# Both pieces of the products of rows 9 to 12 side by side in the fixed opening list of a retention and feed-forward kernel

## The chip, the cores and the metric

The kernel runs on one core of a Trainium2 chip. A core has five engines, each with an instruction stream of its own that it works through in order: PE (TensorE, the matrix products), DVE (VectorE), ACT (ScalarE), POOL (GpSimd) and SP (SyncE, which here only issues DMAs; ACT issues DMAs too). The streams are tied to each other by semaphores. The metric is the device time of one launch in microseconds. In the three timed runs of the kernel before it was 571.28, 571.71 and 572.1 us; the median is 571.71 us.

## The reference

Two stages. A retention layer with 4 sequences, 8 heads, 768 tokens and a head size of 64 keeps a 64x64 state for each sequence and head, and then a feed-forward layer turns the 3072 tokens of 512 values into 2048 values and back:

```python
for t in range(S):
    state = gamma * state + einsum('bhd,bhe->bhde', k[:, :, t], v[:, :, t])
    y[:, :, t] = scale * einsum('bhd,bhde->bhe', q[:, :, t], state)
x = y, heads side by side, as (3072, 512)
h = x @ w_in
g = h * clip(h + 3.0, 0.0, 6.0) / 6.0
out = g @ w_out
```

The two weight matrices arrive as 64-bit floats, and the kernel turns them into 32-bit floats itself, in integer steps.

## The kernel before, in words

Tokens are taken in 24 rows of 128, six rows to a sequence. A row of the retention needs small products on PE, 64x64 each and 4 head pairs times 2 halves at a time: `score` (keys against queries, into bank `sc`), `inner` (weighed scores times values, into bank `y`), `add` (keys times values, added to the running state in bank `uz`) and `past` (the state before times the queries, into `y`). A row from the ninth on has two halves of 64 tokens. The function `later(r)` (line 464) makes the lists for one turn: the last additions and the products of row r-1 with the scores and the first additions of row r. A turn has two pieces. The first piece takes the second additions of row r-1 into `uz` and its first `past` products. The second piece (`chunk_rest`, line 495) has three groups one after another: scores of row r beside `past`; scores beside `inner`; then the first additions of row r, into `uz` again, beside `inner`. Between the pieces ACT must copy `uz` out into an SBUF tile named `state` (`keep`, line 460, traced as L462), because the third group of the second piece writes `uz` anew. The third group of the second piece therefore waits for that copy. After the second piece a second copy is made.

The feed-forward products are tiles `h` (line 505): 512 columns of one unit u of four rows, 12 products per tile, in four PSUM banks that take turns. They need the rows' `y` as x (high and low part) and the weights, which come in as 64-bit words and are converted for a column block j by DVE and ACT steps a, b, e, q, f, w, then split by u (high part, ACT, line 219) and v (low part, DVE, line 222). A finished tile goes through ACT (`relu`, line 512, step r), DVE (`times`, line 516, step g) and a store of 256 KB to device memory, which ACT issues (line 539) just behind a later relu. The tiles g have three buffers, so a relu also waits until the store of the tile three before has landed.

What runs in the opening, and in which order, is a list written out by hand, `HEAD` (lines 57 to 77). Each word is one step of `step()`; PE, DVE, ACT and SP take their instructions in exactly this order. `P9` is the first piece of row 9's turn, `J9` the copy behind it, `Q9` the second piece, `K9` the copy after that; `h1.2` is a quarter of tile (unit 1, column block 2); `r1.2` and `g1.2` are the relu and the product of that tile; `e7` and `u7` are the ACT steps of weight block 7. After the opening, in `steady()`, each row's turn is one `chunk_burst` (line 482): first piece, copy, second piece, copy, without anything between them on PE.

Of the kernel before, what the change touches and what calls it, by code (L numbers as in the profile page):

```python
# [31 lines left out]
def retention_ffn(ctx: ExitStack, tc: tile.TileContext, qkv, w_in, w_out, dvs, dkc, dqc, dmc, tab, out, B, H, S, D):  # L32
# [23 lines left out]
    COPIED = (0, 1, 4, 5)  # L56
    HEAD = """
        L0 L1 F L2 F L3 L4 O0 c0 T0 m0.0 T1 C0 T2 d0 m0.1 C1 T3 C2 N0 O1 x0 c1 U0 d1 m1.0 T4 B0 U1 a0 Y1 b0 e0 m1.1 X0
        q0 N1 f0 F L5 L6 L7 c2 O2 w0 B1 x1 d2 Y2 m2.1 u0 m2.0 U2 a1 N2 B2 l0 X1 b1 T5 C3 c3 O3 x2 d3 Y3 m3.1 m3.0 e1
        U3 l1 N3 B3 q1 C4 O4 c4 x3 f1 F Y4 d4 m4.1 m4.0 X3 U4 X2 v0 O5 B4 w1 C5 N4 l2 c5 a2 Y5 l3 d5 m5.0 x4 e2 s6  # L60
        m5.1 h0.0 c6 b2 N5 f2 d6 q2 F h0.0 u1 m6 p6 x5 h0.0 A6 X4 v1 S7 c7 w2 h0.0 a3 X5 m7 h0.1 u2 b3 l5 y6 h0.1 v2
        B6 e3 q3 p7 h0.1 l4 A7 d7 h0.1 f3 F h0.2 x6 r0.0 w3 i7 X6 u3 y7 h0.2 x7 h0.2 g0.0 X7 v3 h0.2 r0.1 l6 B7 h0.3
        l7 L8 h0.3 a4 h1.0 b4 e4 g0.1 h1.0 r0.2 q4 h1.0 f4 F h1.0 w4 h1.1 g0.2 u4 h0.3 a5 r1.0 v4 h1.1 g1.0 h0.3 b5
        h0.4 r0.3 q5 h0.4 e5 h0.4 f5 F h0.4 g0.3 Q8 L9 w5 a6 h1.1 K8 b6 r0.4 q6 h1.1 u5 P9 e6 h1.2 r1.1 h1.2 J9 g1.1
        h1.2 m8 h1.2 f6 F h1.3 v5 h1.3 w6 h1.3 g0.4 u6 h1.3 r1.2 v6 h1.4 r1.3 a7 h1.4 b7 e7 Q9 g1.2 q7 g1.3 h1.4 f7 F
        h1.4 w7 h1.5 a8 u7 b8 h1.5 e8 q8 h1.5 K9 f8 F L10 r1.4 h0.5 g1.4 h1.5 v7 h1.6 w8 h0.5 a9 u8 h0.5 b9 r1.5 q9
        h0.5 v8 h1.6 g1.5 h1.6 h1.6 P10 r1.6 h1.7 e9 h0.6 J10 f9 F r0.5 h0.6 m9 h1.7 g0.5 h0.6 g1.6 h1.7 w9 h1.7 a10
        b10 h0.6 r1.7 q10 h0.7 u9 e10 Q10 v9 r0.6 f10 F w10 h1.8 a11 u10 h0.7 b11 X8 q11 h0.7 e11 g1.7 h0.7 K10 g0.6
        X9 h1.8 v10 r0.7 h1.8 f11 F L11 h0.8 w11 h0.8 g0.7 h1.8 a12 l8 h0.8 r1.8 h0.8 g1.8 h1.9 r0.8 h1.9 u11 g0.8 e12
        h1.9 v11 h1.9 f12 P11 m10 h1.10 b12 h1.10 q12 F h1.10 l9 h1.10 w12 h1.11 a13 u12 b13 h1.11 J11 v12 r1.9 h1.11  # L70
        e13 g1.9 h1.11 r1.10 q13 Q11 f13 F L12 g1.10 w13 h1.12 X10 m11 h0.9 K11 u13 l10 h1.12 a14 h0.9 b14 e14 q14
        h0.9 r1.11 f14 h1.12 g1.11 P12 v13 h1.12 J12 w14 h0.9 a15 h0.10 u14 b15 r1.12 h0.10 e15 v14 h0.10 r0.9 h0.10
        g1.12 h0.11 r0.10 q15 h0.11 f15 h0.11 g0.9 h0.11 w15 h0.12 g0.10 u15 h0.12 r0.11 v15 h0.12 g0.11 h0.12 Q12
        r0.12 g0.12 h0.13 K12 m12 X11 h0.13 l11 h0.13 h0.13 h0.14 r0.13 h0.14 g0.13 h0.14 h0.14 h0.15 r0.14 h0.15
        g0.14 h0.15 h0.15 h1.13 r0.15 h1.13 g0.15 h1.13 h1.13 h1.14 r1.13 h1.14 g1.13 h1.14 h1.14 h1.15 r1.14 h1.15
        g1.14 h1.15 h1.15 r1.15 g1.15
    """
    BUFS = {"lkt": 1, "lqt": 2, "lvn": 2, "lkn": 1}
    SPARE = ("lkn", "lkt", "lqt", "lqt")
# [832 lines left out]
```

## Time and profile before

| | |
|---|---|
| median of the timed runs | 571.71 us |
| profiled execution | 572.05 us |
| its span, first to last instruction | 570.3 us |
| PE busy | 563.5 us (99%) |
| DVE busy | 429.6 us (75%) |
| ACT busy | 249.2 us (44%) |
| granted TensorE clock, mean | 1.000 |

The span is the part of the execution that the profiler sees; the other 1.75 us lie around it. A busy share is an average over the whole span, and matmuls are pipelined, so a busy PE can still be held up by a few tenths of a microsecond that only the start times show. The trace counts a 64x64 product of the program as two records, so a piece of 16 products shows as 32 records.

The opening lasts from 0 to about 122 us. Its turns of rows 9 to 12 stand at these times on PE: first pieces at 58.05, 77.02, 96.00 and 108.24 us, second pieces at 65.70, 84.00, 102.29 and 118.60 us.

### The profile page before, as it was taken

The numbers are of one execution on the slowest core, as the hardware profiler recorded it, in microseconds if no ns is written. First come the engines' busy times: TensorE is split into PE (matmuls) and PEld (weight loads), VectorE is DVE, ScalarE is ACT, GpSimd is POOL, SyncE is SP. The second block draws the span as 40 slices with busy tenths as digits, with TensorE's granted clock in tenths as the row PEclk, the third lists the DMA queues.
The fourth block names the chain that finished last, engine by engine and source line by source line (L and its number), as shares of the span: only waits on it lengthen the run. The fifth ranks groups of instructions, "written<-read, shape, count | busy, mean of one in ns | idle before, by whom it ended". The sixth has DMA issues, their size and how long they took to land.

```text
span 570.3 us, 11862 instructions
## 1 busy us (share of the span) xinstructions
PE 563.5 (99%) x4832; PEld 462.6 (81%) x4832; DVE 429.6 (75%) x594; ACT 249.2 (44%) x388; POOL 44.2 (8%) x50
## 2 busy tenths in 40 slices
PE   8999999999999999999999999999999999999997
PEld 6777888888888888888888888888888888888885
DVE  5879879942777678887737989679776698676881
ACT  4863434532444443444434654444335443344430
POOL 3001110220111111122000000000000000000000
PEclk9999999999999999999999999999999999999999
DMA  8946787762656666667543485565744747636611
GB/s 314 369 140 220 232 278 228 259 227 92 220 206 223 216 223 215 231 231 260 165 161 115 150 292 189 175 226 167 263 165 132 240 162 258 206 115 189 213 75 74
DMA packets 60626, 115.68 MB, mean 203 GB/s; under 512 B 6166, under 2 KB 6934, under 8 KB 60572
## 3 DMA queue, kind: packets, MB, share of 16 engines
q1 hardware_dynamic: 46304, 89.54, 47.8%
q10 hardware_dynamic: 14268, 25.39, 11.7%
q8 instruction: 38, 0.62, 0.5%
q14 instruction: 16, 0.13, 0.1%
HBM read 83.45 MB, written 31.46 MB: 201 GB/s over the span
## 4 chain that ended last, share of the span: by engine, by line
PE 94%; DVE 3%; DMA 1%; ACT 0%; issue 0%; SPq 0%; DVEq 0%
PE h L505 45%; PE o L782 40%; PE uz L458 3%; PE y L458 3%; PE sc L458 2%; DMA early<-in_qkv 1%; DMA st<-in_w_in 1%; DVE we L200 1%; DVE x L222 0%; DVE am L381 0%; DVE w L222 0%; DVE g L516 0%; DVE wb L187 0%; DVE xr L609 0%; DVE wb L195 0%
## 5 line engine op out<-in xcount | busy, mean ns | idle before, releaser
L505 PE MATMUL h<-x,w 128*128 128x512 f32 x1152 | 270.1, 393 | 0.2
L505 PEld LDWEIGHTS h<-x,w 128*128 128x128 f32 x1152 | 213.9, 188 | 46.4 <-DVE w L222 0.6
L782 PE MATMUL o<-gc,w 128*128 128x512 f32 x1008 | 228.6, 389 | 0.0
L782 PEld LDWEIGHTS o<-gc,w 128*128 128x128 f32 x1008 | 189.2, 188 | 39.3
L512 ACT ACTIVATE g<-h,three 128x512 f32<-128x512 f32 x96 | 65.8, 687 | 109.7 <-PE h L505 81.1
L516 DVE SCALAR_TENSOR_TENSOR g<-g,h 128x512 f32<-128x512 f32 x96 | 65.5, 684 | 56.2 <-ACT g L512 56.0
L219 ACT ACTIVATE gc<-gv 128x1024 fp32r<-128x1024 f32 x48 | 50.9, 1060 | 61.0 <-PE o L782 55.2
L222 DVE TENSOR_TENSOR gc<-gv,gc 128x1024 fp32r<-128x1024 f32 x48 | 58.7, 1222 | 22.5 <-ACT gc L219 22.5
L219 ACT ACTIVATE gc<-spare 128x1024 fp32r<-128x1024 f32 x36 | 38.2, 1061 | 50.3 <-PE o L782 43.3
L222 DVE TENSOR_TENSOR gc<-spare,gc 128x1024 fp32r<-128x1024 f32 x36 | 44.0, 1221 | 10.1 <-ACT gc L219 10.0
L192 ACT ACTIVATE we<-we,ebias 128x512 int32<-128x512 int32 x32 | 23.0, 719 | 17.1 <-DVE we L183 16.3
L219 ACT ACTIVATE w<-ww 128x384 fp32r<-128x384 f32 (+2 forms) x34 | 18.6, 552 | 24.9 <-DVE ww L206 20.6
L200 DVE SCALAR_TENSOR_TENSOR we<-st,we 128x512 int32<-128x512 int32 x32 | 23.0, 720 | 2.3 <-ACT we L192 2.2
L195 DVE SCALAR_TENSOR_TENSOR wb<-st,wb 128x512 f32<-128x512 uint32 x32 | 23.0, 720 | 0.7
L347 POOL TENSOR_TENSOR qs<-qt,dq 128x512 f32<-128x512 f32 x16 | 23.0, 1439 | 6.3 <-DMA dq<-in_decays_q 6.3
L206 DVE SCALAR_TENSOR_TENSOR ww<-wb,we 128x512 f32<-128x512 f32 x32 | 22.9, 715 | 0.8
L462 ACT ACTIVATE state<-uz 128x256 f32<-128x256 f32 x39 | 14.8, 379 | 19.5 <-PE y L458 9.7
L222 DVE TENSOR_TENSOR w<-ww,w 128x384 fp32r<-128x384 f32 (+2 forms) x34 | 20.4, 604 | 1.5 <-ACT w L219 1.4
L136 DVE TENSOR_TENSOR spare<-spare,gv 128x1024 f32<-128x1024 f32 x12 | 14.7, 1223 | 6.1 <-DMA gv<-gd 6.0
L343 POOL TENSOR_TENSOR kn<-kn,ccst 128x512 f32<-128x512 f32 x8 | 9.0, 1128 | 120.9 <-DMA kn<-in_qkv 85.0
L458 PE MATMUL y<-qs,state 64*64 64x64 f32 x480 | 18.3, 222 | 0.0
L458 PE MATMUL y<-am,vn 64*64 64x64 f32 x512 | 18.1, 219 | 0.0
(69 smaller groups left out, 417.9 us busy)
## 6 DMA issues: line engine op xcount, KB each, us to landing
gd<-g ACTq DMA_DIRECT2D x96, 256.0 KB, 2.9
gv<-gd SPq DMA_DIRECT2D x48, 512.0 KB, 4.7
gv<-gd SPq DMA_DIRECT2D x48, 256.0 KB, 3.0
st<-in_w_in SPq DMA_DIRECT2D x32, 256.0 KB, 3.9
st<-in_w_out SPq DMA_DIRECT2D x16, 512.0 KB, 5.8
early<-in_qkv SPq DMA_DIRECT2D x28, 256.0 KB, 4.6
kt<-in_qkv SPq DMA_DIRECT2D x16, 256.0 KB, 3.5
qt<-in_qkv SPq DMA_DIRECT2D x16, 256.0 KB, 3.9
```

The lines of the kernel that those rows point to most:

```text
L192: nc.scalar.activation(out=t["e"], in_=t["e"], func=AF.Relu, scale=8.0, bias=ebias)
L195: nc.vector.scalar_tensor_tensor(out=t["b"].bitcast(F32), in0=lo.bitcast(U32), scalar=2.0**-32, in1=t["b"], op0=ALU.mult, op1=ALU.add)
L200: nc.vector.scalar_tensor_tensor(out=t["e"], in0=hi, scalar=-2147483648, in1=t["e"], op0=ALU.bitwise_and, op1=ALU.bitwise_or)
L206: nc.vector.scalar_tensor_tensor(out=t["w"], in0=t["b"].bitcast(F32), scalar=2.0**-20, in1=t["e"].bitcast(F32), op0=ALU.mult, op1=ALU.mult)
L219: nc.scalar.activation(out=hi, in_=src, func=AF.Copy)
L222: nc.vector.tensor_tensor(out=lo, in0=src, in1=hi, op=ALU.subtract)
L347: nc.gpsimd.tensor_tensor(out=t["qs"], in0=t["qt"], in1=d, op=ALU.mult)
L458: nc.tensor.matmul(out_, lhs, rhs, start=start, stop=True, skip_group_check=True)
L505: nc.tensor.matmul(h, t[:, o, a], xs[u][b][:, k], start=k + n == 0, stop=(k, n) == (NK - 1, 2), skip_group_check=True)
L512: return g, nc.scalar.activation(out=g, in_=h, func=AF.Relu, bias=three).ins
L516: ins = nc.vector.scalar_tensor_tensor(out=g, in0=g, scalar=6.0, in1=h, op0=ALU.min, op1=ALU.mult)
L782: nc.tensor.matmul(acc[i][h] if last else acc[i][:, h], w2c[j][:, RIGHT[i], x, h], gc[:, y, jj], start=j == 0 and n == 0, stop=j == NFP - ...
```

## The change

In the list `HEAD` the words P9, J9, P10, J10, P11, J11, P12 and J12 move to the place just ahead of Q9, Q10, Q11 and Q12. No other word moves against the rest, and nothing is added or taken out. Two lines of the table, before and after (the end of it becomes one line shorter, so that line 505 of the kernel before is line 504 in the changed one, and so on):

```diff
-        h0.4 r0.3 q5 h0.4 e5 h0.4 f5 F h0.4 g0.3 Q8 L9 w5 a6 h1.1 K8 b6 r0.4 q6 h1.1 u5 P9 e6 h1.2 r1.1 h1.2 J9 g1.1
-        h1.2 m8 h1.2 f6 F h1.3 v5 h1.3 w6 h1.3 g0.4 u6 h1.3 r1.2 v6 h1.4 r1.3 a7 h1.4 b7 e7 Q9 g1.2 q7 g1.3 h1.4 f7 F
...
+        h0.4 r0.3 q5 h0.4 e5 h0.4 f5 F h0.4 g0.3 Q8 L9 w5 a6 h1.1 K8 b6 r0.4 q6 h1.1 u5 e6 h1.2 r1.1 h1.2 g1.1 h1.2 m8 h1.2 f6 F h1.3
+        v5 h1.3 w6 h1.3 g0.4 u6 h1.3 r1.2 v6 h1.4 r1.3 a7 h1.4 b7 e7 P9 J9 Q9 g1.2 q7 g1.3 h1.4 f7 F h1.4 w7 h1.5 a8 u7
```

PE at the turn of row 9, before. The `uz` and `y_138<-qs_783,state_765` rows are the end of the first piece, `h_937`, `h_960` and `h_983` are the tiles of unit 1 and blocks 2, 3 and 4, and the `sc` row begins the second piece:

```order
L458 MATMUL uz<-vn_776,kn_778 64x64 x2
L458 MATMUL y_138<-qs_783,state_765 64x64 x2
L505 MATMUL h_937<-x_587,w_24_314 128x512 x12
L505 MATMUL h_960<-x_587,w_24_314 128x512 x6
L505 MATMUL h_960<-x_587,w_56_710 128x512 x6
L505 MATMUL h_983<-x_587,w_56_710 128x512 x6
L458 MATMUL sc<-qt_891,kt_889 64x64 x2
L458 MATMUL y_138<-qs_783,state_908 64x64 x2
```

The same place on PE in the changed kernel, where the three tiles are called `h_921`, `h_942` and `h_965`:

```order
L504 MATMUL h_921<-x_587,w_24_314 128x512 x12
L504 MATMUL h_942<-x_587,w_24_314 128x512 x6
L504 MATMUL h_942<-x_587,w_56_710 128x512 x6
L504 MATMUL h_965<-x_587,w_56_710 128x512 x6
L457 MATMUL uz<-vn_776,kn_778 64x64 x2
L457 MATMUL y_138<-qs_783,state_765 64x64 x2
...
L457 MATMUL sc<-qt_891,kt_889 64x64 x2
L457 MATMUL y_138<-qs_783,state_908 64x64 x2
```

The first piece has moved behind 30 products of h tiles, and its last rows now touch the second piece.

ACT at the same place, before. `state_946<-uz` is the copy J9, `w_56_710<-ww_968` the high part of weight block 6, `g_978` and `g_987` the relus of blocks 2 and 3 of unit 1, the two DMA rows stores, `we_989` step e of weight block 7 and `w_103_1060` the high part of block 7:

```order
L512 ACTIVATE g_941<-h_818,three 128x512
L462 ACTIVATE state_946<-uz 128x256
L219 ACTIVATE w_56_710<-ww_968 128x4x128
L512 ACTIVATE g_978<-h_937,three 128x512
L539 DMA gd_67<-g_941 128x512
L539 DMA gd_69<-g_912 128x512
L512 ACTIVATE g_987<-h_960,three 128x512
L192 ACTIVATE we_989<-we_989,ebias 128x512
L219 ACTIVATE w_103_1060<-ww_1058 128x4x128
```

ACT there in the changed kernel, with `state_995` for J9, `g_925`, `g_960` and `g_969` for the three relus and `we_971` for step e7:

```order
L511 ACTIVATE g_925<-h_818,three 128x512
L218 ACTIVATE w_56_710<-ww_950 128x4x128
L511 ACTIVATE g_960<-h_921,three 128x512
L538 DMA gd_67<-g_925 128x512
L538 DMA gd_69<-g_912 128x512
L511 ACTIVATE g_969<-h_942,three 128x512
L191 ACTIVATE we_971<-we_971,ebias 128x512
L461 ACTIVATE state_995<-uz 128x256
L218 ACTIVATE w_103_1060<-ww_1058 128x4x128
```

The copy has moved behind six instructions of ACT: a weight split, two relus, two stores and an exponent step.

ACT at the turn of row 10, in the changed kernel. `g_1190` is the relu of block 7 of unit 1, the two DMA rows are stores, then come step u and step e of weight blocks 9 and 10, and `state_1217<-uz` is J10:

```order
L511 ACTIVATE g_1190<-h_1148,three 128x512
L538 DMA gd_69<-g_1161 128x512
L538 DMA gd_70<-g_1145 128x512
L218 ACTIVATE w_103_1060<-ww_1178 128x4x128
L191 ACTIVATE we_1183<-we_1183,ebias 128x512
L461 ACTIVATE state_1217<-uz 128x256
```

The copy has moved behind these five instructions and behind one more relu that stands ahead of them.

## Rows read from the trace of the kernel before

**Rows 1.** The page: the chain of work that ended last and its shares of the span by engine.

```profile
PE 94%; DVE 3%; DMA 1%; ACT 0%; issue 0%; SPq 0%; DVEq 0%
```

**Rows 2.** The same chain in order of time, from 52 us on: start us, length us, what. All pieces left out are PE too, up to the last one shown.

```profile
52.43 2.56 PE h L505 x10
...
338.22 228.49 PE o L782 x1008
```

**Rows 3.** Waits of PE over the span, the one row in which it waits for a copy of the state: for whom, us in total, times, longest.

```profile
PE y L458 <- ACT state L462: 0.2, 1, 0.2
```

**Rows 4.** The timeline of PE at the turn of row 9: the start of the first piece, the h tiles between, the start of the second piece, the start of its third group, the next h tile. Columns: start us, length us, engine, line, operation.

```profile
58.05 0.27 PE L458 MATMUL uz<-vn,kn 64*64 64x64 f32 x2
58.68 7.09 PE L505 MATMUL h<-x,w 128*128 128x512 f32 x30
65.70 0.27 PE L458 MATMUL sc<-qt,kt 64*64 64x64 f32 x2
66.68 0.24 PE L458 MATMUL uz<-vn,am 64*64 64x64 f32 x2
67.28 9.81 PE L505 MATMUL h<-x,w 128*128 128x512 f32 x42
```

**Rows 5.** The timeline of PE at one turn of the steady part, where nothing stands between the pieces: first piece, its last addition, third group of the second piece, next h tile; and the third group and next h tile of a second such turn, which began at 181.53 us.

```profile
155.24 0.27 PE L458 MATMUL uz<-vn,am 64*64 64x64 f32 x2
155.69 0.23 PE L458 MATMUL uz<-vn,am 64*64 64x64 f32 x2
156.68 0.24 PE L458 MATMUL uz<-vn,kn 64*64 64x64 f32 x2
157.28 0.96 PE L505 MATMUL h<-x,w 128*128 128x512 f32 x3
...
183.01 0.27 PE L458 MATMUL uz<-vn,kn 64*64 64x64 f32 x2
183.63 0.72 PE L505 MATMUL h<-x,w 128*128 128x512 f32 x2
```

**Rows 6.** The copy of ACT inside those two turns.

```profile
156.02 0.38 ACT L462 ACTIVATE state<-uz 128x256 f32<-128x256 f32 x1
...
182.32 0.38 ACT L462 ACTIVATE state<-uz 128x256 f32<-128x256 f32 x1
```

**Rows 7.** The timeline of ACT from the copy J9 to step e7 (ACTq rows are DMA issues by ACT's queue). In brackets: the idle time of the engine before it, and what ended it.

```profile
59.19 0.39 ACT L462 ACTIVATE state<-uz 128x256 f32<-128x256 f32 x1
62.59 0.63 ACT L219 ACTIVATE w<-ww 128x512 fp32r<-128x512 f32 x1 [3.01 <-DVE ww L206]
62.77 0.33 ACTq L539 DMA_DIRECT2D gd<-g  x1
...
63.19 0.39 ACTq L539 DMA_DIRECT2D gd<-g  x1
66.59 0.69 ACT L512 ACTIVATE g<-h,three 128x512 f32<-128x512 f32 x1 [2.79 <-DMA gd<-g]
67.18 0.71 ACT L192 ACTIVATE we<-we,ebias 128x512 int32<-128x512 int32 x1
```

**Rows 8.** The stores that ACT issued from 62 to 68 us, and from 55 to 125 us: time to landing, us, min/median/max.

```profile
DMA to landing us min/median/max: 3.9/3.9/3.9
...
DMA to landing us min/median/max: 2.0/3.8/5.9
```

**Rows 9.** The timeline of PE at the turn of row 10: first piece, h tiles, second piece, next h tile.

```profile
77.02 0.27 PE L458 MATMUL uz<-vn,am 64*64 64x64 f32 x2
77.65 6.42 PE L505 MATMUL h<-x,w 128*128 128x512 f32 x27
84.00 0.27 PE L458 MATMUL sc<-qt,kt 64*64 64x64 f32 x2
85.57 10.49 PE L505 MATMUL h<-x,w 128*128 128x512 f32 x45
```

**Rows 10.** The timeline of ACT there: the relu ahead of the two stores, the second of the two issues by itself, step u9 and step e10.

```profile
82.74 0.69 ACT L512 ACTIVATE g<-h,three 128x512 f32<-128x512 f32 x1 [3.12 <-PE h L505]
83.22 1.09 ACTq L539 DMA_DIRECT2D gd<-g  x1
84.36 0.63 ACT L219 ACTIVATE w<-ww 128x512 fp32r<-128x512 f32 x1 [0.93 <-DVE wb L195]
84.90 0.71 ACT L192 ACTIVATE we<-we,ebias 128x512 int32<-128x512 int32 x1
```

**Rows 11.** The second issue of the two other pairs of stores that ACT issues back to back in the opening.

```profile
70.38 0.44 ACTq L539 DMA_DIRECT2D gd<-g  x1
...
118.66 1.03 ACTq L539 DMA_DIRECT2D gd<-g  x1
```

**Rows 12.** The turns of rows 11 and 12. First PE and ACT at row 11, from the timeline: the start of the second piece and the issue of a store just behind it in time. Then from the chain of waits the first piece of row 12 (start us, length us) and the start of its second piece, and from ACT's timeline the relu ahead of the pair of stores there.

```profile
102.29 0.27 PE L458 MATMUL sc<-qt,kt 64*64 64x64 f32 x2
...
102.32 0.33 ACTq L539 DMA_DIRECT2D gd<-g  x1
...
108.24 0.61 PE y L458 x16
...
118.60 0.20 PE sc L458 x2
...
118.22 0.69 ACT L512 ACTIVATE g<-h,three 128x512 f32<-128x512 f32 x1 [0.95 <-DMA gd<-g]
```

More of the change, by code (lines that the diff above doesn't have):

```diff
@@ L58, in retention_ffn @@
         L0 L1 F L2 F L3 L4 O0 c0 T0 m0.0 T1 C0 T2 d0 m0.1 C1 T3 C2 N0 O1 x0 c1 U0 d1 m1.0 T4 B0 U1 a0 Y1 b0 e0 m1.1 X0
[L59 to L62, printed above, removed]
@@ L63, in retention_ffn @@
-        l7 L8 h0.3 a4 h1.0 b4 e4 g0.1 h1.0 r0.2 q4 h1.0 f4 F h1.0 w4 h1.1 g0.2 u4 h0.3 a5 r1.0 v4 h1.1 g1.0 h0.3 b5
-        h0.4 r0.3 q5 h0.4 e5 h0.4 f5 F h0.4 g0.3 Q8 L9 w5 a6 h1.1 K8 b6 r0.4 q6 h1.1 u5 P9 e6 h1.2 r1.1 h1.2 J9 g1.1
-        h1.2 m8 h1.2 f6 F h1.3 v5 h1.3 w6 h1.3 g0.4 u6 h1.3 r1.2 v6 h1.4 r1.3 a7 h1.4 b7 e7 Q9 g1.2 q7 g1.3 h1.4 f7 F
-        h1.4 w7 h1.5 a8 u7 b8 h1.5 e8 q8 h1.5 K9 f8 F L10 r1.4 h0.5 g1.4 h1.5 v7 h1.6 w8 h0.5 a9 u8 h0.5 b9 r1.5 q9
-        h0.5 v8 h1.6 g1.5 h1.6 h1.6 P10 r1.6 h1.7 e9 h0.6 J10 f9 F r0.5 h0.6 m9 h1.7 g0.5 h0.6 g1.6 h1.7 w9 h1.7 a10
@@ L68, in retention_ffn @@
[L68 to L76, printed above, removed]
+        q0 N1 f0 F L5 L6 L7 c2 O2 w0 B1 x1 d2 Y2 m2.1 u0 m2.0 U2 a1 N2 B2 l0 X1 b1 T5 C3 c3 O3 x2 d3 Y3 m3.1 m3.0 e1 U3
@@ new lines, in retention_ffn @@
+        l1 N3 B3 q1 C4 O4 c4 x3 f1 F Y4 d4 m4.1 m4.0 X3 U4 X2 v0 O5 B4 w1 C5 N4 l2 c5 a2 Y5 l3 d5 m5.0 x4 e2 s6 m5.1
+        h0.0 c6 b2 N5 f2 d6 q2 F h0.0 u1 m6 p6 x5 h0.0 A6 X4 v1 S7 c7 w2 h0.0 a3 X5 m7 h0.1 u2 b3 l5 y6 h0.1 v2 B6 e3 q3
+        p7 h0.1 l4 A7 d7 h0.1 f3 F h0.2 x6 r0.0 w3 i7 X6 u3 y7 h0.2 x7 h0.2 g0.0 X7 v3 h0.2 r0.1 l6 B7 h0.3 l7 L8 h0.3
+        a4 h1.0 b4 e4 g0.1 h1.0 r0.2 q4 h1.0 f4 F h1.0 w4 h1.1 g0.2 u4 h0.3 a5 r1.0 v4 h1.1 g1.0 h0.3 b5 h0.4 r0.3 q5
+        h0.4 e5 h0.4 f5 F h0.4 g0.3 Q8 L9 w5 a6 h1.1 K8 b6 r0.4 q6 h1.1 u5 e6 h1.2 r1.1 h1.2 g1.1 h1.2 m8 h1.2 f6 F h1.3
@@ new lines, in retention_ffn @@
+        v5 h1.3 w6 h1.3 g0.4 u6 h1.3 r1.2 v6 h1.4 r1.3 a7 h1.4 b7 e7 P9 J9 Q9 g1.2 q7 g1.3 h1.4 f7 F h1.4 w7 h1.5 a8 u7
+        b8 h1.5 e8 q8 h1.5 K9 f8 F L10 r1.4 h0.5 g1.4 h1.5 v7 h1.6 w8 h0.5 a9 u8 h0.5 b9 r1.5 q9 h0.5 v8 h1.6 g1.5 h1.6
+        h1.6 r1.6 h1.7 e9 h0.6 f9 F r0.5 h0.6 m9 h1.7 g0.5 h0.6 g1.6 h1.7 w9 h1.7 a10 b10 h0.6 r1.7 q10 h0.7 u9 e10 P10
+        J10 Q10 v9 r0.6 f10 F w10 h1.8 a11 u10 h0.7 b11 X8 q11 h0.7 e11 g1.7 h0.7 K10 g0.6 X9 h1.8 v10 r0.7 h1.8 f11 F
+        L11 h0.8 w11 h0.8 g0.7 h1.8 a12 l8 h0.8 r1.8 h0.8 g1.8 h1.9 r0.8 h1.9 u11 g0.8 e12 h1.9 v11 h1.9 f12 m10 h1.10
@@ new lines, in retention_ffn @@
+        b12 h1.10 q12 F h1.10 l9 h1.10 w12 h1.11 a13 u12 b13 h1.11 v12 r1.9 h1.11 e13 g1.9 h1.11 r1.10 q13 P11 J11 Q11
+        f13 F L12 g1.10 w13 h1.12 X10 m11 h0.9 K11 u13 l10 h1.12 a14 h0.9 b14 e14 q14 h0.9 r1.11 f14 h1.12 g1.11 v13
+        h1.12 w14 h0.9 a15 h0.10 u14 b15 r1.12 h0.10 e15 v14 h0.10 r0.9 h0.10 g1.12 h0.11 r0.10 q15 h0.11 f15 h0.11 g0.9
+        h0.11 w15 h0.12 g0.10 u15 h0.12 r0.11 v15 h0.12 g0.11 h0.12 P12 J12 Q12 r0.12 g0.12 h0.13 K12 m12 X11 h0.13 l11
+        h0.13 h0.13 h0.14 r0.13 h0.14 g0.13 h0.14 h0.14 h0.15 r0.14 h0.15 g0.14 h0.15 h0.15 h1.13 r0.15 h1.13 g0.15
@@ L77, in retention_ffn @@
+        h1.13 h1.13 h1.14 r1.13 h1.14 g1.13 h1.14 h1.14 h1.15 r1.14 h1.15 g1.14 h1.15 h1.15 r1.15 g1.15
     """
```

## The prediction

> **What bounds the kernel now.** I read the chain of waits first. PE holds 94% of it [rows 1], and from 52.43 us to the end every piece of it is a PE piece: first the h tiles and small products, then from 338.22 us the output products [rows 2]. The list of what PE waited for comes next: in the whole span it waited for a copy of the state once, 0.2 us long [rows 3]. So whatever is put into PE's stream after 52 us, work or a wait, lengthens the kernel by just as much, and whatever is taken out shortens it. No slack further on can take it back. The timelines of PE and ACT around the four turns give the sizes.
>
> **What the change takes away.** Each of the four first pieces stands between h tiles, and going from h tiles to 64x64 products and back costs something. The first piece of row 9 takes 58.68 - 58.05 = 0.63 us of PE, the second 67.28 - 65.70 = 1.58, together 2.21 [rows 4]. In the steady part, where the pieces touch, both take 157.28 - 155.24 = 2.04 us [rows 5]. Joining them saves 0.17 us a turn; row 10 gives the same (0.63 + 1.57 = 2.20) [rows 9]. For four turns that is 0.68 us at most, 0.12% of the time. The number of products is unchanged, and no DMA moves on SP or POOL: their instructions stand as before.
>
> **What it adds: a wait for the copy.** The third group of the second piece overwrites the bank that the copy reads. Before, the copy had 6.5 us (row 9: ACT made it at 59.19, the third group came at 66.68) [rows 4, 7]. Now it has only the first two groups of the second piece: in the steady turn the third group starts 156.68 - 155.24 = 1.44 us after the first piece began, and the last addition of that piece starts at 0.45 us and takes 0.23 [rows 5]. The copy takes 0.38 us. In the first steady turn it ended at 156.40 and the third group began at 156.68, on its beat; in the second it ended at 182.70 and the group began at 183.01 [rows 5, 6]. I take 0.28 to 0.31 us from the copy's end to PE. So the copy must start no later than 1.44 - 0.38 - 0.29 = 0.77 us after the first piece, and its data are there at 0.68. That suffices only if ACT is free at that moment. ACT takes its instructions in order, so what counts is what now stands ahead of the copy.
>
> **Row 9.** Ahead of it now stand the weight split u6, the relu of tile h1.2, two stores, the relu of h1.3 and step e7. In the trace the split starts at 62.59, having waited 3.01 us for DVE, the stores are issued at 62.77 and 63.19, and the relu of h1.3 starts only at 66.59, after 2.79 us of waiting for a store of g to land: it needs the buffer that the store issued at 62.77 empties, and the stores of this stretch took 3.9 us [rows 7, 8]. Step e7 follows at 67.18. None of this waits for the first piece of row 9, whose old place was 58.05, and the h tiles that the relus read only come 0.63 us sooner. So I leave these ACT times as they are. The next ACT instruction follows e7 after 67.18 - 66.59, about 0.6 us: the copy runs from 67.79 to 68.17 and PE can go on at 68.46. PE itself gets to the joined pieces at 65.70 - 0.63 = 65.07 and to the third group at 65.07 + 1.44 = 66.51. It waits 1.95 us. From the third group to the next h tile takes 0.60 us [rows 4], so that tile starts at 69.06 against 67.28 before: **+1.78 us**, the 0.17 saved included. Behind the waiting product on PE stands everything else, all h tiles to come; behind the copy on ACT stands u7, which before started only at 69.38 and so has room. This is the term on which the forecast rests.
>
> **Row 10.** Let T be the start of the joined pieces. Now the copy stands behind the relu of h1.7, two stores, u9 and e10. The relu waits for PE and starts where it did relative to the small products, 84.00 - 82.74 = 1.26 us ahead of T; the second store's issue took 1.09 us, from 83.22 to 84.31, and u9 followed at 84.36, e10 at 84.90 [rows 9, 10]. With these rows u9 starts at T + 0.36, e10 at T + 0.90, the copy at T + 1.51; it ends at T + 1.89 and PE goes on at T + 2.18, 0.74 us late. But the second issue of such a pair took 0.39, 0.44, 1.09 and 1.03 us in four cases [rows 7, 10, 11], and I see no reason in the trace for the difference. With 0.39 the copy waits for the additions alone, starts about 0.8 us after T, and PE waits some 0.05. I take the mean of the four, 0.74: 0.35 less than the row, so a wait of 0.39 us, and with the 0.17 saved **+0.22 us**, ends -0.12 and +0.57.
>
> **Rows 11 and 12.** At row 11 the copy stands behind a store whose issue was at 102.32 while the second piece began at 102.29 [rows 12]. There the joined pieces would start at 102.29 - 0.63 = 101.66, the copy at about 102.7, and PE would wait 0.26 us if ACT came as late relative to PE as before. But PE is now some 2 us later, and ACT only partly follows, since DVE, which paces it there, does not wait for PE. I take a wait of 0.04 us: **-0.13**, ends -0.17 and +0.09. At row 12 no additions stand in the first piece, and the copy (of a state that nobody reads) stands behind a relu that waited for a store until 118.22 and behind a pair of stores, the second 1.03 us long [rows 11, 12]. With ACT as late as before the copy would end near 120.1, PE could go on at 120.38, and would be ready at 118.60 - 0.61 + 1.44 = 119.43, a wait of 0.95; with PE 1.5 to 2 us later it does not wait at all. I take **-0.17**, other end +0.78.
>
> **The sum.** 1.78 + 0.22 - 0.13 - 0.17 = +1.70 us, on the profiled execution 572.05 + 1.70 = 573.75. The profiled one stands 0.34 us above the median of the runs; on the median 571.71 it is 573.41, and I predict 573.4.
>
> **A page that gives another size.** The stores of row 9's stretch took 3.9 us, beside loads [rows 8]. The Trainium skill, DMA: Bandwidth & Descriptors, section "Anatomy of one DMA — SWDGE (gpsimd) path", fits about 2.0 us plus the bytes over 436 GB/s for one transfer on that path; for 256 KB I work out an estimate of 2.6 us from that page. By that estimate the relu of h1.3 would start at 65.4, PE would wait about 0.75 us instead of 1.95, and the sum would be +0.5 us, 572.2, a time within the rival of the early store below. The trace disagrees here, where the store took 3.9 us; its shortest store, 2.0 us, lies under the page's figure, its median of 3.8 over it.
>
> **The rivals.** *The store of row 9's stretch lands early* (other side). If the landing takes the trace's shortest 2.0 us instead of 3.9, the relu starts at 64.8, the copy near 66.0, and PE goes on at 66.66: a wait of 0.15, row 9 gives -0.02. Then PE comes to rows 10 to 12 barely later than before, and their waits stand: with the short issue +0.05 - 0.17 at row 10, about 0 at row 11, and at row 12 anything from -0.17 to +0.78. In the good case the sum is -0.3 us, 571.4, not slower; with row 12's wait it is +0.6, 572.3. The point from which it decides: a landing 0.56 us sooner (3.3 us) brings +1.70 under 1.14, one 1.70 us sooner (2.2 us) brings it to nothing. For it: the stores spread from 2.0 to 5.9 us [rows 8]. Against it: the loads that share the DMA with this store are issued as before, and by the same instructions.
>
> *The late issues fall together.* Row 10 pays its full 0.57 and row 11 its 0.09: 1.78 + 0.57 + 0.09 - 0.17 = +2.27, 574.0. For it: row 10's own issue was the long one. Against it: two of the four pairs were short.
>
> *The copy is never late*, or the change does only what it says: the copies get to ACT in time and just the four joins are left, -0.68 us, 571.0. For it speaks the steady part, where the same order costs nothing [rows 5, 6]. Against it speaks the order of ACT together with the store's landing [rows 7]; it would need ACT to take the copy ahead of a waiting relu.
>
> *More is late than I see*: a wait of PE of more than 3 us in all, because the moved waits shift a load or a store behind the small products. +3 us, 574.7. Nothing in the rows asks for it.
>
> **How the numbers follow.** About 0.2%, 1.14 us, is what a measurement of this kernel can tell from no change. The forecast with its spread (row 9 decides, +1.2 to +2.1) gets 0.45, the late issues 0.20, the early store 0.24, the copy never late 0.05, more than I see 0.06. Slower by over 0.2% are nearly all of the forecast's cases (0.42 of 0.45), the late issues and the last: 0.68, and 0.02 of the early store with row 12's wait at its end make 0.70. Within 0.2% are the early store and most of the rest: 0.27. Faster by over 0.2% would need more than the joins can give; 0.03 for what I overlook. The range reaches from 572.1 (early store with a wait at row 12) to 574.5 (late issues and somewhat more); the forecast's own is 572.9 to 573.8.
>
> **What would show it.** Right: in the list of what PE waited for a new row names the copy (ACT state) with about 2 us in its longest case; in PE's timeline near 66.5 us a gap of about 2 us ahead of the third group; on ACT the relu at 66.6, e7 at 67.2 and the copy at 67.8, in a row; and joined pieces at row 11 of about 2.05 us. Wrong: the copy of row 9 before 66.3, or a gap at row 12 larger than that at row 9. If PE's gap is there and the time unchanged, then something after 70 us gave it back, and my first paragraph is wrong.

## The result, and the profile after

The changed kernel took 575.50 us, the median of eleven executions (573.67 to 578.40); the kernel before, run beside it, took 571.84. The ratio is 1.0065, interval 1.0048 to 1.0083: slower, by about 3.7 us where 1.7 were forecast. The direction was right, the time fell above the range. One of the eleven executions of the kernel before took 801.3 us, and the ratio leaves it out. The execution with a profile took 576.05 us, its span 574.3 against 570.3.

The chain of waits gives the first sign. Where PE held 94% before and the DMAs 1% [rows 1], PE now holds less and the DMAs more:

```profile
PE 89%; DMA 5%; DVE 3%; issue 1%; ACT 0%; SPq 0%; ACTq 0%; DVEq 0%
```

The stretches' table says where, here for the stretch of 55 to 130 us alone. Its columns are the length, then busy time and number of instructions of PE, of PE's weight loads, of DVE, ACT and POOL, and last the granted TensorE clock, the DMA engines' busy share and GB/s. First the kernel before, then the changed one:

```profile
55.00:130.00 75.00, 75.00 (x822) 61.14 (x823) 59.01 (x97) 32.76 (x59) 12.86 (x10) 1.00 0.71 241
```

```profile
55.00:130.00 75.00, 71.48 (x809) 58.91 (x809) 58.45 (x96) 32.26 (x58) 9.82 (x8) 1.00 0.69 232
```

PE was busy without a break before; now it stands idle for 3.52 us of the 75. PE's timeline of the changed kernel at the four turns (start us, length us, engine, line, operation, in brackets the idle time ahead and what ended it):

```profile
65.53 0.27 PE L457 MATMUL uz<-vn,kn 64*64 64x64 f32 x2
...
68.68 0.27 PE L457 MATMUL uz<-vn,am 64*64 64x64 f32 x2 [1.52 <-issue]
...
69.30 0.96 PE L504 MATMUL h<-x,w 128*128 128x512 f32 x3
...
85.19 0.27 PE L457 MATMUL uz<-vn,am 64*64 64x64 f32 x2
...
87.23 0.98 PE L504 MATMUL h<-x,w 128*128 128x512 f32 x3
...
103.13 0.33 PE L457 MATMUL uz<-vn,kn 64*64 64x64 f32 x4
103.68 0.27 PE L457 MATMUL y<-qs,state 64*64 64x64 f32 x2 [0.22 <-DVE x L221]
...
107.07 0.27 PE L457 MATMUL uz<-vn,am 64*64 64x64 f32 x2 [1.78 <-issue]
107.70 1.67 PE L504 MATMUL h<-x,w 128*128 128x512 f32 x6
...
121.56 0.51 PE L457 MATMUL y<-qs,state 64*64 64x64 f32 x10
...
123.58 1.66 PE L504 MATMUL h<-x,w 128*128 128x512 f32 x6
```

Row 9 waits 1.52 us at its third group, row 10 takes 87.23 - 85.19 = 2.04 us and waits for nothing, row 12 takes 2.02. Row 11, where I had forecast 0.04 us of waiting, waits 0.22 + 1.78: its pieces last 4.57 us instead of 2.04. The releaser is written "issue"; that it is the copy is seen on ACT. ACT at row 9, which answers to [rows 7]:

```profile
63.28 0.64 ACT L218 ACTIVATE w<-ww 128x512 fp32r<-128x512 f32 x1 [3.28 <-DVE ww L205]
63.47 0.33 ACTq L538 DMA_DIRECT2D gd<-g  x1
...
67.01 0.69 ACT L511 ACTIVATE g<-h,three 128x512 f32<-128x512 f32 x1 [2.52 <-DMA gd<-g]
67.59 0.71 ACT L191 ACTIVATE we<-we,ebias 128x512 int32<-128x512 int32 x1
68.21 0.37 ACT L461 ACTIVATE state<-uz 128x256 f32<-128x256 f32 x1
```

This is the forecast's picture: the relu waits for a store, e7 and the copy follow, and PE goes on 0.10 us after the copy's end. ACT ahead of row 11's copy:

```profile
95.21 0.69 ACT L511 ACTIVATE g<-h,three 128x512 f32<-128x512 f32 x1 [0.80 <-DVE g L515]
97.57 0.33 ACTq L538 DMA_DIRECT2D gd<-g  x1
97.94 0.63 ACT L218 ACTIVATE w<-ww 128x512 fp32r<-128x512 f32 x1 [2.04 <-DMA st<-in_w_in]
...
104.17 0.64 ACT L218 ACTIVATE w<-ww 128x512 fp32r<-128x512 f32 x1 [4.98 <-DVE ww L205]
...
105.27 0.71 ACT L191 ACTIVATE we<-we,ebias 128x512 int32<-128x512 int32 x1
105.88 0.68 ACT L511 ACTIVATE g<-h,three 128x512 f32<-128x512 f32 x1
106.16 0.33 ACTq L538 DMA_DIRECT2D gd<-g  x1
106.59 0.39 ACT L461 ACTIVATE state<-uz 128x256 f32<-128x256 f32 x1
```

Look at the store at 97.57. It writes g away, and the bracket on the row behind it says that ACT sat idle for 2.04 us until a load of weights (`st<-in_w_in`) landed, whose data this store does not touch. The chain in order of time shows the same:

```profile
91.56 0.33 SPq L156
...
91.94 5.55 DMA st<-in_w_in
97.57 0.33 ACTq L538
...
97.94 0.64 ACT w L218
...
105.29 1.78 issue
107.07 0.27 PE uz L457 x2
```

The instruction list of the built program, which gives for each instruction the semaphores it waits for, tells why. The DMAs of SP and ACT report their end through eight semaphores that they share (DMAHW0 to 7), and a DMA may have to wait until an earlier one on its semaphore has ended. ACT's rows around this store, before and after:

```
105 L539 DMA gd_70<-g_1311 128x512 [waits DMAHW7_49,DVE_49]
106 L512 ACTIVATE g_1364<-h_1334,three 128x512 [waits DMAHW2_49,PE_49]
107 L539 DMA gd_71<-g_1353 128x512 [waits DVE_49]
```

```
105 L538 DMA gd_70<-g_1311 128x512 [waits DMAHW0_49,DVE_49]
106 L511 ACTIVATE g_1364<-h_1334,three 128x512 [waits DMAHW4_49,PE_49]
107 L538 DMA gd_71<-g_1353 128x512 [waits DMAHW3_49,DVE_49]
```

Order and operands are the same; only the semaphores have moved, and the store of tile (1,8), `gd_71<-g_1353`, has got one on which a load came before it, the one whose 5.55 us begin at 91.94. In the list of e5 below, where P10 and J10 stand ahead of u9 and e10, the store waits for DVE alone again. The same shift changes the waits of thirteen more DMA issues of SP and ACT, some now behind a load and some no longer. Of ACT's idle times from 55 to 125 us only the 2.04 us above are put down to a load.

### The profile page after: what moved, and what is told of

It reads as the page before. It is cut to its first block, busy times and chain, and to the rows that moved or that the text cites. A ratio compares the mean times of both kernels' runs of the same rounds, so it can differ in the third digit from the quotient of the medians.

```text
span 574.3 us, 11864 instructions
## 1 busy us (share of the span) xinstructions
PE 563.1 (98%) x4832; PEld 463.2 (81%) x4832; DVE 426.1 (74%) x594; ACT 249.1 (43%) x388; POOL 43.0 (7%) x50
## 4 chain that ended last, share of the span: by engine, by line
PE 89%; DMA 5%; DVE 3%; issue 1%; ACT 0%; SPq 0%; ACTq 0%; DVEq 0%
PE h L504 43%; PE o L781 40%; DMA early<-in_qkv 3%; PE uz L457 2%; PE y L457 2%; PE sc L457 2%; DMA st<-in_w_in 2%; DVE g L515 0%; DVE w L221 0%; SPq L156 0%; DVE x L221 0%; DVE we L199 0%; DVE wb L194 0%; DVE ww L205 0%; DVE wb L186 0%
## 5 line engine op out<-in xcount | busy, mean ns | idle before, releaser
L346 POOL TENSOR_TENSOR qs<-qt,dq 128x512 f32<-128x512 f32 x16 | 21.5, 1341 | 6.9 <-DMA dq<-in_decays_q 6.7
L138 DVE TENSOR_TENSOR spare<-gv 128x1024 f32<-128x1024 f32 x12 | 14.7, 1221 | 4.8 <-DMA gv<-gd 4.8
```

Source lines behind the costliest of these rows:

```text
L346: nc.gpsimd.tensor_tensor(out=t["qs"], in0=t["qt"], in1=d, op=ALU.mult)
```

## The experiments

Each was timed beside the kernel before on the same chip. The kernel before took 572.10 us in the median beside e1 to e4, 572.13 beside e5 to e8 and 572.27 beside e9 to e12. The ratio is to that time, with its 95% interval. Waits are those over 0.15 us of PE at rows 9 to 12 in the one profiled execution. The last column is from that execution too: the time from the first score product of row 8 to that of row 13, less the 87.68 us of the kernel before in its one profile. These are its two ends there, in PE's timeline:

```profile
54.92 1.15 PE L458 MATMUL sc<-qt,kt 64*64 64x64 f32 x32
...
142.60 0.22 PE L458 MATMUL sc<-qt,kt 64*64 64x64 f32 x1
```

| run | median us (executions) | ratio, interval | PE waits at row: us | rows 8 to 13 us |
|---|---|---|---|---|
| e1, row 9 | 573.75 (8) | 1.0027, 1.0018 to 1.0037 | 9: 1.49 | +1.42 |
| e2, row 10 | 572.35 (11) | 1.0007, 0.9998 to 1.0016 | 10: 0.20 | +0.24 |
| e3, rows 9, 11, 12 | 574.04 (10) | 1.0038, 1.0023 to 1.0053 | 9: 1.38; 11: 0.20 | +0.87 |
| e4, rows 9, 10, 12 | 575.06 (6) | 1.0060, 1.0041 to 1.0079 | 9: 1.91; 12: 0.45 | +1.68 |
| e5, change, J10 ahead of u9, e10 | 573.50 (5) | 1.0031, 1.0019 to 1.0044 | 9: 1.67; 11: 1.48 | +2.10 |
| e6, and J9 ahead of r1.3, e7 | 571.59 (11) | 0.9995, 0.9986 to 1.0004 | none | -1.48 |
| e7, rows 10, 11 | 575.48 (5) | 1.0057, 1.0045 to 1.0069 | 10: 0.39; 11: 0.43, 1.77 | +2.63 |
| e8, all copies earlier | 571.01 (12) | 0.9986, 0.9977 to 0.9994 | none | -1.47 |
| e9, row 11 | 572.28 (11) | 0.9997, 0.9988 to 1.0006 | none | -0.26 |
| e10, e7 with J10 ahead of u9, e10 | 571.94 (11) | 0.9995, 0.9986 to 1.0003 | 11: 0.21 | -0.28 |
| e11, change, J11 ahead of r1.10 | 574.01 (9) | 1.0034, 1.0021 to 1.0047 | 9: 1.84; 11: 0.55; 12: 0.19 | +1.79 |
| e12, the change again | 574.86 (4) | 1.0048, 1.0035 to 1.0061 | 9: 2.23; 11: 1.30 | +2.47 |

The changed kernel of the section before has +2.80 in that column (55.60 to 146.08).

**e1: row 9 alone**, against the kernel before.

```diff
-u5 P9 e6 h1.2 r1.1 h1.2 J9 g1.1
+u5 e6 h1.2 r1.1 h1.2 g1.1
...
-e7 Q9 g1.2
+e7 P9 J9 Q9 g1.2
```

> Only P9 and J9 are moved to Q9; rows 10 to 12 as before. Theory A (two causes: the late copy of row 9, and at row 11 a late copy behind a store that waits for a load): +1.3 to +1.8 us, about 573.3, all of it in one gap of PE of 1.5 to 2 us ahead of the third group of row 9; no gap after it. Theory B (each row costs by itself, row 11 most): the same here. If the row-9 gap were given back later: no change.

573.75, 1.65 us above its kernel before, with the one wait at row 9. That agrees with the term I forecast at +1.78.

**e2: row 10 alone.**

```diff
-P10 r1.6 h1.7 e9 h0.6 J10 f9
+r1.6 h1.7 e9 h0.6 f9
...
-u9 e10 Q10
+u9 e10 P10 J10 Q10
```

> Only P10 and J10 are moved to Q10. In the built program this alone makes the store of tile (1, 8) wait for a load of weights of block 11, which it does not do in the kernel before. Theory A: the store and ACT behind it are held up about 2 us near 95 to 98 us as in the changed kernel, but the copy of row 11 stands far ahead of its reader, so PE loses nothing: -0.2 to +0.6 us, 571.6 to 572.4. Theory A2 (the store's wait costs by itself): +1.5 to +2.2 us, with a gap of PE after 97 us. Theory B: -0.2.

+0.25 us, not to be told from nothing, with 0.20 us of waiting. The store of tile (1,8) already carries the new semaphore here. ACT around this store, DVE's product named in the bracket, and the two loads that SP issued just before (length of the issue in ns, min/median/max, starts of the first and the last, then us to landing), the second of them the one that the store waits for:

```profile
94.79 0.33 ACTq L539 DMA_DIRECT2D gd<-g  x1
95.17 0.63 ACT L219 ACTIVATE w<-ww 128x512 fp32r<-128x512 f32 x1 [0.87 <-DVE g L516]
...
94.33 0.69 DVE L516 SCALAR_TENSOR_TENSOR g<-g,h 128x512 f32<-128x512 f32 x1 [1.06 <-ACT g L512]
...
L157 SPq DMA_DIRECT2D st<-in_w_in x2: 328/376/425, 90.4 to 90.8; - x2
...
DMA to landing us min/median/max: 3.7/3.8/3.9
```

The bracket names DVE, but that product ran until 95.02, past the store's issue. The load issued at 90.8 landed 3.9 us later, at 94.7, and the store went out at 94.79. So ACT was held by the load here too, 0.87 us long, and PE lost nothing by it: J11, at its old place, was made at 100.57, 2 us ahead of the product that needs it (102.92).

**e3: the change without row 10**, against the changed kernel.

```diff
-r1.6 h1.7 e9 h0.6 f9
+P10 r1.6 h1.7 e9 h0.6 J10 f9
...
-u9 e10 P10 J10 Q10
+u9 e10 Q10
```

> Rows 9, 11 and 12 joined, row 10 as before; the store of tile (1, 8) then waits for DVE alone, as in the kernel before. Theory A: row 9's gap of 1.5 to 2 us and nothing of note at row 11 (a wait under 0.4 us): +1.0 to +1.6 us, about 573.1. Theory B: the gap of 1.8 us at row 11 stays, +3.3 us, about 575. Theory C (PE's delay at row 9 moves loads and stores so that row 11 is late): as B.

With J10 at its old place the store of tile (1,8) waits for no load, and the wait of 1.78 us at row 11 is 0.20, although row 11 is joined. So the joined pair of row 11 alone is not what costs. The time is 1.94 us above its kernel before, a little over theory A's range.

**e4: the change without row 11.**

```diff
-f12 m10
+f12 P11 m10
...
-h1.11 v12
+h1.11 J11 v12
...
-q13 P11 J11 Q11
+q13 Q11
```

> Rows 9, 10 and 12 joined, row 11 as before: the store of tile (1, 8) still waits for the load, but the copy of row 11 is made early. Theory A: the 2 us hold of ACT is there and PE does not feel it: +1.0 to +1.6 us, about 573.1. Theory A2: +3.3 us. Theory B: +1.2.

ACT was held 1.38 us by the load, and row 11 did not wait. So the hold alone costs PE nothing there either. Yet the time is 575.06, 2 us over what theory A gave, and by the time alone theory A2 fits better. Against A2 stand e2 and the profile, which has no gap of PE at row 11. The profiled execution took 574.74: its row 8 begins 0.84 us later than before, a difference that comes by chance (e12), and rows 8 to 13 add 1.68, with waits of 1.91 at row 9 and 0.45 at row 12. Two of the six executions, 575.39 and 578.01, had a granted clock of 0.997. So the median says less here than the profile.

**e5: the change, with row 10's copy two words earlier.**

```diff
-h0.7 u9 e10 P10 J10 Q10
+h0.7 P10 J10 u9 e10 Q10
```

> The changed kernel with one difference: the copy of row 10 stands ahead of u9 and e10 instead of behind them (the four joined pairs stay). In the built program the store of tile (1,8) then no longer waits for the load of weights that ScalarE was held by for 2.04 us in the changed kernel. Theory A (ScalarE's hold by that load pushes row 11's copy, which stands behind another store, past the end of the ready work): the wait of 1.78 us at row 11 is gone (under 0.3), ScalarE's idle time ahead of that store is gone, row 9's wait of about 1.5 stays; time 573.4 to 574.2. Theory B (row 11's wait comes from its own place behind r1.10 and e13, whatever happens on ScalarE before): the wait at row 11 stays above 1.3 and the time stays at 575 to 575.7.

The median is 573.50, as theory A said, 2.0 us under the changed kernel's 575.50 and 1.4 under its 574.86 (e12), and ACT's idle time for the load is gone. The profile does not follow theory A: row 11 waits 1.48 us, in an execution of 574.50, the second longest of the five. ACT there, then GpSimd and VectorE, same columns:

```profile
102.96 0.68 ACT L511 ACTIVATE g<-h,three 128x512 f32<-128x512 f32 x1
104.62 0.33 ACTq L538 DMA_DIRECT2D gd<-g  x1
105.05 0.38 ACT L461 ACTIVATE state<-uz 128x256 f32<-128x256 f32 x1 [1.42 <-DVE g L515]
```

```profile
101.64 1.47 POOL L346 TENSOR_TENSOR qs<-qt,dq 128x512 f32<-128x512 f32 x1
```

```profile
101.88 1.51 DVE L186 TENSOR_SCALAR wb<-st 128x512 int32<-128x512 int32 x1
...
103.92 0.68 DVE L515 SCALAR_TENSOR_TENSOR g<-g,h 128x512 f32<-128x512 f32 x1
```

The store ahead of the copy waits for the product g, and that stands behind a DVE step that took 1.51 us (0.42 as a rule) and ended 0.28 us after GpSimd's product did. The Trainium skill, SBUF — State Buffer, section "Who interferes with whom", says that VectorE and GpSimd share a pair of ports, which one of them can hold for a whole instruction while the other stands still; these rows agree. So row 11's copy can be late with no load involved: one store more ahead of it ties it to DVE. That GpSimd is the cause is argued and not shown, since no run leaves its product out, and a DVE step is as long in e6 (1.75 us at 100.20), behind the product g there, where nothing waits.

**e6: the same, with row 9's copy earlier too** (against e5).

```diff
-r1.3 a7 h1.4 b7 e7 P9 J9 Q9
+a7 h1.4 b7 P9 J9 r1.3 e7 Q9
```

> The changed kernel with two copies a few words earlier: that of row 9 ahead of r1.3 and e7, that of row 10 ahead of u9 and e10; all four pairs stay joined. Theory A (all of the loss is copies late behind ScalarE's work on other tiles): no wait of TensorE over 0.3 us at rows 9 to 12, every joined pair about 2.04, and the time 571.2 to 572.2, no longer above the kernel before. Theory D (joining the pairs costs something by itself, in the start or in what follows, since three of the profiles with joined pairs begin 0.6 to 0.8 us later): the waits are gone but the time stays at 572.8 or more.

No wait at any row, 571.59: the whole loss is gone with four pairs still joined. Theory D falls. The wait of 1.48 us at row 11 is gone as well, although only row 9's copy moved against e5, so in e5 PE's delay at row 9 had a part in it.

**e7: rows 10 and 11 alone.** The edit of e2 and that of row 11 (below, e9).

> Only rows 10 and 11 as in the change, rows 9 and 12 as before; the store of tile (1,8) waits for the load as in the changed kernel. Theory A: the hold on ScalarE (about 0.9 us where row 9 was left alone, 2.04 in the changed kernel) now has row 11's late copy behind it; a wait at row 11 of 0.5 to 1.8 us, no other wait over 0.3, time 572.6 to 573.9. Theory C (row 9's delay is needed: it is what shifts the load and the tiles against each other): the hold is absorbed as in the run with row 10 alone, no wait over 0.3 at row 11, time 571.9 to 572.5.

The run that decides most: without row 9 the loss is 3.35 us, nearly that of the whole change. Theory C falls, and theory A's time was too low. In the profiled execution (575.76) rows 8 to 13 add 2.63 us, with waits of 0.39, 0.43 and 1.77; turns after row 13 add 0.89, one of them a wait of 0.47 at 265.8 us. Such late turns belong to no one edit: e8, e9 and e11 have waits of 0.34, 0.41 and 0.58 between 261 and 265 us. ACT, to be compared with the changed kernel's rows above:

```profile
96.93 0.33 ACTq L538 DMA_DIRECT2D gd<-g  x1
97.30 0.63 ACT L218 ACTIVATE w<-ww 128x512 fp32r<-128x512 f32 x1 [2.08 <-DMA st<-in_w_in]
...
103.14 0.63 ACT L218 ACTIVATE w<-ww 128x512 fp32r<-128x512 f32 x1 [4.59 <-DVE ww L205]
...
105.56 0.38 ACT L461 ACTIVATE state<-uz 128x256 f32<-128x256 f32 x1
```

DVE between the two splits has one long step, 0.69 us in e10:

```profile
100.24 1.66 DVE L194 SCALAR_TENSOR_TENSOR wb<-st,wb 128x512 f32<-128x512 uint32 x1
```

**e8: all copies earlier.** That of e6 and, for rows 11 and 12:

```diff
-r1.10 q13 P11 J11 Q11
+q13 P11 J11 r1.10 Q11
...
-h1.12 w14
+h1.12 J12 w14
...
-h0.12 P12 J12 Q12
+h0.12 P12 Q12
```

> All four pairs joined, and each copy a few words earlier than in the change: row 9's ahead of r1.3 and e7, row 10's ahead of u9 and e10, row 11's ahead of r1.10, row 12's at its old place ahead of w14 with its first piece still joined. The store of tile (1,8) waits for no young load. Theory A: no wait over 0.2 us at any of the four rows, 0.17 us saved at each, 571.2 to 571.7, that is 0.4 to 0.9 under the kernel before. Theory D (the saving of the joined pair is taken back elsewhere, or joining costs something by itself): 572.0 or more.

571.01: 1.1 us under the kernel before, interval 0.3 to 1.3, and faster than both kernels. PE at rows 9 and 11 in this run, each pair 2.04 us from its first piece to the next h tile, with no bracket:

```profile
64.58 0.27 PE L457 MATMUL uz<-vn,kn 64*64 64x64 f32 x2
...
66.62 0.73 PE L504 MATMUL h<-x,w 128*128 128x512 f32 x2
...
100.46 0.27 PE L457 MATMUL uz<-vn,kn 64*64 64x64 f32 x2
...
102.50 0.73 PE L504 MATMUL h<-x,w 128*128 128x512 f32 x2
```

Each pair takes what the steady turns said [rows 5], once the copies come in time. But rows 8 to 13 are 1.47 us shorter than before, and 1.48 in e6, where four joins of 0.17 would give 0.68. At row 9 it is plain: from row 8's first score product to row 9's it is 10.78 or 10.79 us in the five profiles where the pair stands apart and 10.44 or 10.45 in the nine where it is joined. The rest of the saving lies in the h tiles around the piece.

**e9: row 11 alone.**

```diff
-f12 P11 m10
+f12 m10
...
-h1.11 J11 v12
+h1.11 v12
...
-q13 Q11
+q13 P11 J11 Q11
```

> Only row 11 as in the change, rows 9, 10 and 12 as before; the store of tile (1,8) waits for no load. Theory S (the copy of row 11 is late whenever the work that ScalarE does ahead of it is late, and only the hold of 2 us by the load makes it so in most executions): no wait of TensorE over 0.3 us at row 11, time 571.8 to 572.5. Theory T (its place behind one more store is enough; the hold by the load only adds to it): a wait of 0.8 to 1.6 us at row 11, time 572.7 to 573.6.

572.28 against 572.27, no wait: theory S. Its place behind one more store costs nothing by itself in the median of eleven executions.

**e10: e7 with row 10's copy earlier**, the edit of e5.

> The run with rows 10 and 11 alone (575.48) with one difference: the copy of row 10 stands ahead of u9 and e10, so that the store of tile (1,8) waits for no load. Theory S: ScalarE's idle time of 2.08 us ahead of that store is gone, the waits of 0.39, 0.43 and 1.77 us go with it, and the time is 571.6 to 572.6. Theory T: the two waits of 0.39 and 0.43 go, that at row 11 stays at 0.8 to 1.6, and the time is 572.7 to 573.8.

571.94: two words of the list take back 3.5 us. ACT in this run, where the same store goes out at once and the weight split follows 2.4 us sooner than in e7:

```profile
94.33 0.69 ACT L511 ACTIVATE g<-h,three 128x512 f32<-128x512 f32 x1 [1.73 <-DMA gd<-g]
94.36 0.33 ACTq L538 DMA_DIRECT2D gd<-g  x1
94.92 0.62 ACT L218 ACTIVATE w<-ww 128x512 fp32r<-128x512 f32 x1
...
99.84 0.64 ACT L218 ACTIVATE w<-ww 128x512 fp32r<-128x512 f32 x1 [3.69 <-DVE ww L205]
...
102.68 0.38 ACT L461 ACTIVATE state<-uz 128x256 f32<-128x256 f32 x1 [0.44 <-PE y L457]
```

The split is 3.30 us sooner at its next block (99.84 against 103.14), the copy 2.88. Of the 3.30, 2.38 are there at the split behind the store; the rest is about the DVE step that took 1.66 us in e7 and takes 0.69 here. Theory S holds. The edit also takes u9 and e10 from ahead of the copy of row 10; that was worth no more than row 10's wait of 0.39. It also changes what seven other DMA issues wait for; no idle time of ACT there is put down to another load in either run.

**e11: the change with row 11's copy earlier.**

```diff
-r1.10 q13 P11 J11 Q11
+q13 P11 J11 r1.10 Q11
```

> The changed kernel with one difference: the copy of row 11 stands ahead of the tile step r1.10, so ahead of one relu and one store that waits for a product of VectorE. The store of tile (1,8) still waits for the load. Theory S and T alike: the wait of 1.78 us at row 11 shrinks to 0.2 to 0.6, because ScalarE reaches the copy about 1.3 us sooner; row 9's wait of about 1.5 stays; time 573.8 to 574.5. Theory U (the copy follows VectorE's chain, which the hold makes late anyway): the wait stays above 1.2 and the time at 575 or more.

574.01 and 0.55 us at row 11, as theories S and T had it, while ACT was still held 1.62 us by the load. The hold does harm only where a copy that PE needs soon stands behind it.

**e12: the changed kernel again.**

> The changed kernel once more, for a second profile. If the waits are of the program and not of one execution: again about 1.5 us at row 9 and over 1.3 at row 11, ScalarE held about 2 us by the load; time 574.5 to 576. If the start that came 0.7 us later in the first profile belongs to the change, the products of row 8 begin at 55.4 to 55.8 again; if it is chance, anywhere from 54.4 to 55.8.

574.86, waits of 2.23 and 1.30 us, ACT held 1.72 us. The waits belong to the program, though their sizes differ. The start does not: the products of row 8 began at 54.21 us here and at 55.60 in the first profile, and over fourteen profiles of all kernels anywhere from 54.21 to 55.76.

## Why the prediction was wrong

**What bounds.** Right: PE's idle time comes back in the spans. In the first profile row 8 begins 0.68 us later than before, rows 8 to 13 add 2.80 and the turns after them 0.55, together +4.0 as measured; in the second it is -0.71 + 2.47 + 0.46 = +2.2, as measured.

**The joins, -0.68.** Right in direction, too small in size: the pair takes 2.04 us in e8, where nothing waits, but rows 8 to 13 show about 0.37 us a join, 1.48 in all. I took the time of the pieces alone and left out what a piece set apart costs the h tiles around it. The kernel e8 is 0.3 to 1.3 us faster than before.

**Row 9, +1.78.** Right in mechanism and close in size: +1.65 alone, with waits between 1.38 and 2.23 us (1.95 forecast) in the seven profiles that have it as in the change. The store that the relu waits for did not land early: in the changed kernel the relu began 3.54 us after its issue (63.47 to 67.01), 3.82 before. The 2.6 us that the prediction worked out are of transfers that GpSimd issues; ACT issues this one. Two small sizes were off against each other: PE goes on 0.10 us after the copy and not 0.29, but a wait costs some 0.2 us more than the gap that the profile shows. From row 9's first score product to row 10's it is 17.92 us in e8 and 0.21 to 0.23 more than that and the gap together in the five profiles that wait at row 9 with row 10 joined (19.65 with 1.52 in the changed kernel).

**Row 10, +0.22.** Within its ends alone: +0.25, which is not clear of nothing, with a wait of 0.20. In both profiles of the change it waited for nothing, as the forecast had it for a short issue. But what its copy does elsewhere was missing from it.

**Row 11, -0.13.** This is the step that failed. I forecast 0.04 us of waiting; the two profiles of the change show 2.00 and 1.30. Alone it is near right (e9: +0.01); together with row 10 it is +3.1 (e7 against e2). I had written that ACT there is paced by DVE and does not wait for PE, and took ACT's times of the kernel before, because "no DMA moves on SP or POOL: their instructions stand as before". I compared the order of the instructions and not what they wait for. The copy of row 10 shifted the DMA semaphores, a store of ACT then waited about 2 us for a load, DVE's chain of weight steps fed by ACT came 2 to 3 us later (e7 against e10), and the copy of row 11, which this same change had put at the end of that stretch, came late by as much. Neither half costs by itself (e2, e4 at row 11, e9). The ends I gave, -0.17 and +0.09, left no room for it, although by my own sum the copy had no slack left; in e5 a row that is held by no load is late by 1.48 us.

**Row 12, -0.17.** Right in the profile of the change (2.02 us for the pair); 0.45 of waiting in e4 and 0.19 in e11 lie inside its other end.

**The rivals.** The one called "more is late than I see" comes nearest: PE waits more than 3 us in all because a store moved. What moved it was its semaphore, and not a wait of PE as I had it. I gave it 0.06 and said that nothing in the rows asks for it. The rows do not, but the waits of the built program did, and they were there to be read. The signs were mixed. The relu, e7 and the copy came in a row and PE's gap at row 9 was there, if shorter. The joined pieces of row 11, which were to take about 2.05 us, took 4.57. And no new row of waits names the copy: it says "issue", and a row with ACT's state that did appear, 1.5 us long, belongs to the first 50 us.

**What stays open.** The sum of the parts run alone is 1.65 + 0.25 + 0.01 us; the change measured +3.7 and, the second time, +2.6. Rows 8 to 13 of its two profiles give +2.80 and +2.47, and the waits (3.52 and 3.53), 0.2 us more for each wait and four joins at -0.37 make them up to within 0.2; for e4, e5 and e11 the same sum holds to within 0.1. So the median of 575.50 holds about 1 us that is not in these rows. The seven of its eleven executions with a granted clock of 0.999 or more have a median of 574.33, the other four lie at 575.55 and above. Why PE's clock falls in some executions, and whether the waits bring it about, is not shown.

## What to carry to other kernels

When an instruction moves in a program whose DMAs share completion semaphores, compare the waits of every instruction in the built program, not only the order: a store can come to wait for a load that it has nothing to do with. A copy that PE needs within a microsecond goes ahead of every step on its engine that waits for a DMA or for another engine's product, which here turned a change of +3.7 us into one of -1.1. Where a term leaves a copy no slack, its range has to hold every engine that could be late, not just the one in the row.

## What the runs showed of the hardware that I had not expected

ACT stood idle for 2.04 us at a store that waited for a load, through a shared semaphore alone; of the 5.55 us from the start of that load's issue to its landing, 2.07 were SP's issue, where in e2 the issue took 0.42 and the hold was 0.87. A piece of 64x64 products set apart from its neighbour cost about 0.37 us, of which its own time shows only 0.17 (e6, e8). After the copy's end PE went on within 0.10 us (68.58 to 68.68; 106.98 to 107.07), against the 0.28 to 0.31 that I took from the steady turns, where PE was on its beat and not waiting for the copy. And the executions of the change spread wider than those of the kernel before (573.67 to 578.40): the four with a mean granted clock of 0.997 took 575.55 to 578.40, the seven with 0.999 or 1.000 573.67 to 576.05. None of the 73 executions of the kernel before in the three series went under 0.999. Of the 58 executions of the runs in whose profile PE waited over 1.2 us at once, ten went under 0.999; of the 56 of the other runs, one did. No profile was taken in such an execution, so where the clock fell is not shown.
